# Score costs in the plan, fillers in score banks, 48-column chain matmuls, bf16 sums of heads and softmax steps on POOL in a two-layer decode kernel

## The chip, the cores and the metric

The kernel runs on one core of a Trainium2 chip. That core has five engines with a queue each: TensorE (PE, with its weight loads shown as PEld), VectorE (DVE), ScalarE (ACT), GpSimd (POOL) and SyncE (SP), which here only issues DMAs. Each queue is worked off in order; the engines wait for each other through semaphores. The metric is the device time of one execution in microseconds, lower is better.

## The reference

Eight sequences (rows) decode one token through four blocks: attention, MLP, the same attention, the same MLP. Attention has 16 query heads on 8 kv heads of size 256 over a cache of 4096 positions, and needs all of K and V (268 MB) in each of the two layers; the kernel keeps some units of K and V on the chip from a row's first layer to its second. Cut to what matters:

```python
def _A_ref(x, k_cache, v_cache, wq, wo):
    q = (x @ wq).reshape(B, Sq, 16, 256).transpose(0, 2, 1, 3)
    k = jnp.repeat(k_cache, 2, axis=1); v = jnp.repeat(v_cache, 2, axis=1)
    p = softmax(einsum("bhqd,bhkd->bhqk", q, k) * 256 ** -0.5)
    return einsum("bhqk,bhkd->bhqd", p, v).transpose(0, 2, 1, 3).reshape(B, Sq, 4096) @ wo
def _B_ref(x, w1, w2, w3, w4):        # x: (B, 1, 448)
    hs = (shifted gelu(layernorm(x) @ w1)) @ w2       # all shifted away: one position
    x1 = x + hs
    return x1 + gelu(layernorm(x1) @ w3) @ w4
x = x + _A_ref(layernorm(x), ...)
x = x + _B_ref(layernorm(x), ...)
x = x + _A_ref(layernorm(x), ...)
x = x + _B_ref(layernorm(x), ...)
```

With one position the shift by 1 or 2 places moves all of `h` out, so `hs` is zero and w1 and w2 are not read.

## The kernel before

**A plan makes the order.** The body first lists every operation with its engine, a duration, the keys it reads and writes, the PSUM banks it touches and a priority (`Plan.op`). `Plan.schedule` then goes through them by time and writes out one queue for each engine; `synchronise` puts in the semaphore waits. So a changed duration or a changed column count moves instructions in all queues. For PE an operation has two durations (clock warm and cold), the columns it streams and its number of matmuls. Where PE would be idle, the plan puts fillers in: matmuls of 512 columns on the identity, whose result nobody reads, as long as the columns of the last 3.413 us stay under `TARGET` (or `HOT`) and a bank of the four `psT` is free.

**The unit of work is a head**: one kv head with its two query heads, 8 heads x 8 rows x 2 layers = 128. `front(layer, b, h)` does:
- load K in four units of 512 KB, of which one DMA takes up to four; the buffer `kv` holds 30 units;
- transpose K on PE (L1185) into one of four `psT` banks, evicted by DVE (L1168) or ACT (L1169), whichever the plan finds free;
- scores (L999): matmuls of 512 columns into one of two score banks `psS`, four in the four row groups of the output at a time;
- the softmax: the maximum over the bank (L1020, DVE), `pw` (L1022, DVE) masks it by query head, an all-reduce over partitions on POOL gives `gm` (L1025), two small DVE steps make the bias `nb` (L1030, L1032), ACT takes exp with its row sum `lr` (L1035), PE turns `pr` into columns (`turn_p`, L1042), DVE copies them to `pT` (L1046), makes `rs` out of `lr` (L1050), POOL all-reduces it to `Db` (L1052), DVE takes the reciprocal `rc` (L1054).

`back(layer, b, h)` loads V, accumulates p times V in `psP` (L1078) in four row groups, copies the result to `oS` in f32 (L1089), sums the row groups with f32 matmuls (`sum_mm`, L1095) and scales by `rc` into `oA` (L1099). After the seventh head of a row `wo_rows` (L1119) applies wo to seven heads, after the eighth `wo_mm` to the last; then comes the MLP of the row (`mlp`, L825 to L941), whose result `x2c` gives the queries of the second layer (`second_queries`, L1246). Heads of the next rows are put around it.

**Queues.** POOL's queue has the two all-reduces of each head and the copies of layer 0's queries into `qz` (L966). The small matmuls of the chain (queries, MLP, wo) repeat their columns: `QW`, `HW` = 24 and `YW` = 12 columns are streamed where one is needed.

Of the kernel before, what the change touches and what calls it, by code (L numbers as in the profile page):

```python
# [6 lines left out]
P = 128  # L7
B = 8
D = 448
HKV = 8  # L10
DH = 256
F = 1792
NC5 = 5
# [22 lines left out]
BACKS = (0, 3, 6)  # L36
MIX = "KKKKKFFF"
QFIRST = 1
QW, HW, YW = 24, 24, 12
SC = 456  # L40
NQZ = 8
YC = 8
WO = 8
O2 = 0

# [29 lines left out]
class Plan:  # L75

    WIN, COLS, TARGET = 3.413, 3000, 3500

    HOT = 3500


    ISSUE, LEAD = 4.0, 5.0
# [375 lines left out]
def bass_interleave_layers__gqa_block_cached__mixer_s_mlp__decode_kernel(  # L460
# [410 lines left out]
    def mlp(src, skey, n, dst, dkeys):  # L871
# [48 lines left out]
        def y_mm(t):  # L920
            last = None
            for mt in range(NC5):
                for fc in range(14):
                    r = hT[:, fc * n:(fc + 1) * n]
                    r = r if yw == n else bcast(r, yw // n, 1)
                    last = dup(t, ch, yc + mt * yw, yw, w4_sb, fc * D, mt, r, fc == 0, fc == 13)
            return last
        pe(y_mm, 70, rd=["hT"] + W4, wr=[kb], banks=[bk], width=yw)
        ps4 = ch[:, yc:yc + NC5 * yw].rearrange("p (a n) -> p a n", n=yw)[:, :, 0:n]
        dv(lambda v: v.scalar_tensor_tensor(dst, ps4, 0.5, base[:, :, 0:n], ALU.mult, ALU.add),  # L930
           rd=[kb, "base"] + [("base", r) for r in range(1, n) if few], wr=dkeys, banks=[bk])

    def dup(t, dst, at, n, w, a, mt, rhs, start, stop):

# [20 lines left out]
    def front(layer, b, h, prio=None):  # L955
# [26 lines left out]
        for u in range(4):  # L982
            if u in fresh:
                for pc in range(2):
                    bank = transpose_piece(ks[u], pc, u in hold)
                    if u in hold:
                        held.setdefault(u, []).append(bank)

            if u % 2 == 0:
                continue  # L990

            def sc(t, u=u):
                last = None
                w = 2 - 2 * (u // 2)
                for c in range(2):
                    for g4 in range(4):
                        q = ks[u - 1 + g4 // 2]
                        r = 32 * g4
                        last = t.matmul(ps[r:r + 4, :], qz[zi][:, c, w:w + 4],  # L999
                                        slot_ap(q, g4 % 2 * 1024, 1024)[:, c:1024:2],  # L1000
                                        start=(u < 2 and c == 0), stop=(u >= 2 and c == 1),
                                        skip_group_check=True, tile_position=(0, r))
# [17 lines left out]
        plan.op("dve", lambda v: v.tensor_reduce(pm[nm][:, :], ps[:, :], axis=AX.X, op=ALU.max), 0.62,  # L1020
                "max", rd=scs, wr=[("pm", nm)], banks=[sk], prio=hi)
        plan.op("dve", lambda v: v.tensor_scalar(pw[nm][:, :], other[:, :], pm[nm][:, 0:1], 0.0, ALU.add,  # L1022
                                                 ALU.add), 0.1,
                "max", rd=[("pm", nm), "other"], wr=[("pw", nm)], prio=hi)
        plan.op("pool", lambda gp: gp.partition_all_reduce(gm[nm][:, :], pw[nm][:, :], P, RO.max),  # L1025
                0.46, "max", rd=[("pw", nm)], wr=[("gm", nm)], prio=hi)
# [3 lines left out]
        plan.op("dve", lambda v: v.tensor_tensor(nb[nm][:, 1:2], gm[nm][:, 1:2], eb[ei][:, 1:2], ALU.mult), 0.1,  # L1030
                "max", rd=[("gm", nm), ("eb", ei)], wr=[("nb1", nm)], prio=hi)
        plan.op("dve", lambda v: v.scalar_tensor_tensor(nb[nm][:, 0:1], gm[nm][:, 0:1], eb[ei][:, 0:1],  # L1032
                                                        nb[nm][:, 1:2], ALU.mult, ALU.add), 0.1,
                "max", rd=[("gm", nm), ("eb", ei), ("nb1", nm)], wr=[("nb", nm)], prio=hi)
        plan.op("act", lambda a: a.activation(pr[:, :], ps[:, :], ACT.Exp, bias=nb[nm][:, 0:1], scale=scale,  # L1035
                                              accum_out=lr[nm][:, 0:1]), 0.62, "exp",
                rd=[("nb", nm)] + scs + fk, wr=["pr", ("lr", nm)], banks=[sk], prio=hi)
# [7 lines left out]
        pe(turn_p, 4, rd=["pr", "selS"], wr=scs, banks=[sk], name="pturn", prio=hi)  # L1045
        plan.op("dve", lambda v: v.tensor_copy(  # L1046
            pT[nr][:, :, :].rearrange("p (x s) j -> p x s j", s=4),
            ps[:, 0:64].rearrange("p (s x j) -> p x s j", s=4, j=2)), 0.17, "exp", rd=scs,
            wr=[("pT", nr, 0), ("pT", nr, 1)], banks=[sk], prio=hi)
# [8 lines left out]
    def back(layer, b, h):  # L1058
# [12 lines left out]
        for u in range(4):  # L1071
# [26 lines left out]
        pe(sum_mm, 8, rd=["oS", "sel_f"], wr=["o2"], banks=[M], name="osum", prio=hi)  # L1098
# [14 lines left out]
        if k == HKV - 1:  # L1113
            def wo_rows(t):
                last = None
                for n, x in enumerate(heads[:HKV - 1]):
                    for i in range(4):
# [16 lines left out]
            def turn(t):  # L1134
                last = None
                for mt in range(NC5):
                    for w in range(2):
                        last = dup(t, psM, YC + mt * YW, YW, oW, w * D, mt,
                                   bcast(sel[:, 0:1], YW, 1), w == 0, w == 1)
                return last  # L1140
            pe(turn, 10, rd=["hb", "g1", "g2", "hT", "sel"], wr=["psM"], banks=[M], name="turn",
               prio=hi, width=YW)
            dv(lambda v: v.tensor_tensor(acc[layer][:, :], xin, psM[:, YC:YC + NC5 * YW:YW], ALU.add),
               rd=["psM", xk], wr=[ak], banks=[M], name="acc", prio=hi)
        if k == HKV:
            def wo_mm(t):
                last = None
                for mt in range(NC5):
                    for i in range(4):
                        last = dup(t, psM, YC + mt * YW, YW, wo_sb, (4 * h + i) * D, mt,  # L1150
                                   bcast(oT[:, i % 2, i // 2:i // 2 + 1], YW, 1), i == 0,
                                   i == 3)
# [64 lines left out]
    def mid(b, heads):  # L1217

        src = x2c[b % 2]
        mlp(x1c[b % 2], ("x1", b), 1, src[:, :, 0:1], [("x2", b)])  # L1220
        sums(src, ("x2", b), 1, SC + 53)
        second_queries(b, heads[0], None, lambda: dv(
            lambda v: v.tensor_single_scalar(mom2[b % 2][:, :], psM[:, SC + 53:SC + 56], 1.0 / D, ALU.mult),
            rd=["psM"], wr=[("mom2", b)], banks=[M]))
        for h in heads[1:]:
            second_queries(b, h, None)
# [224 lines left out]
```

## Time and profile before

| | |
|---|---|
| median of 3 runs | 1138.31 us (1125.2 to 1138.76) |
| profiled execution | 1128.62 us, span 1126.8 us |
| mean granted TensorE clock | 0.851 |
| bytes moved by DMA | 440.39 MB, mean 391 GB/s |
| POOL all-reduce gm (L1025) | 128 times, mean 354 ns |
| POOL all-reduce Db (L1052) | 128 times, mean 398 ns |
| POOL copy qz (L966) | 64 times, mean 189 ns |
| DVE pw, nb, nb, rs (L1022, L1030, L1032, L1050) | 128 times each, mean 222, 153, 218, 227 ns |
| PE filler (L1392) | 87 times, mean 488 ns |

The profile page lists busy time by engine, the span in 40 slices with a digit for the busy tenths, the chain of work that ended last (followed back from the end through whatever released each step), and groups of equal instructions by line, with the idle time of the engine ahead of them and what ended it. "issue" names idle time in which the engine waited for nothing that the profile shows. L numbers are lines of the kernel before.

### The profile page before, as it was taken

What the parts mean: (1) busy time and instruction counts of PE and PEld (TensorE: products, weight loads), DVE (VectorE), ACT (ScalarE), POOL (GpSimd) and SP (SyncE); (2) the same over time, 40 slices, a digit from 0 to 9 for tenths busy, and PEclk for the clock granted to TensorE, in tenths of its full rate; (3) what the DMA queues carried; (4) which work ended last, traced back from release to release, by engine and by line L of the source; (5) the groups of instructions that cost most, each with busy time, mean ns of one, the idle gap of its engine ahead of it and who ended that gap; (6) DMA issues with size and microseconds to landing.
All of it is one profiled execution on the core that took longest, in us unless ns stands there. A gap on an engine that the chain in (4) does not pass through costs nothing.

```text
span 1126.8 us, 30990 instructions
## 1 busy us (share of the span) xinstructions
PE 962.0 (85%) x13744; PEld 674.1 (60%) x13744; DVE 648.1 (58%) x2055; ACT 286.9 (25%) x578; POOL 109.3 (10%) x347
## 2 busy tenths in 40 slices
PE   5798888988888988888988888888898997898998
PEld 4466546665566755665556655656555774575664
DVE  4357445665556745576466655666555664466562
ACT  1133112231123402243022321233122340133230
POOL 0100011000101101001010101100011010101010
PEclk9789759888789968899599886999778996689698
DMA  9999999988999999999999989999999998999894
GB/s 352 409 425 405 390 393 427 426 344 316 400 427 424 417 342 426 425 425 398 347 425 425 425 355 363 426 425 421 372 400 426 424 379 316 424 421 383 318 406 178
DMA packets 47430, 440.39 MB, mean 391 GB/s; under 512 B 5040, under 2 KB 8256, under 8 KB 16960
## 3 DMA queue, kind: packets, MB, share of 16 engines
q1 hardware_dynamic: 47296, 438.41, 95.5%
q8 instruction: 108, 1.77, 0.6%
q14 instruction: 26, 0.21, 0.0%
HBM read 438.38 MB, written 0.01 MB: 389 GB/s over the span
## 4 chain that ended last, share of the span: by engine, by line
PE 69%; DVE 15%; DMA 7%; ACT 5%; issue 3%; POOL 1%; POOLq 0%; ACTq 0%
PE psT L1185 27%; PE psS L999 12%; PE psP L1078 11%; PE psM L1095 6%; DMA kv<-in_A_v_cache_dram 4%; ACT pr L1035 4%; DVE pm L1020 4%; DMA kv<-in_A_k_cache_dram 3%; PE psM L825 3%; PE psT L1392 2%; DVE oS L1089 2%; DVE kv L1168 2%; PE psM L938 2%; PE psM L1119 2%; PE psM L941 2%
## 5 line engine op out<-in xcount | busy, mean ns | idle before, releaser
L1185 PE MATMUL psT<-ident_f,kv 128*128 128x128 f32 x2816 | 384.2, 291 | 2.9 <-DMA kv<-in_A_k_cache_dram 2.8
L1185 PEld LDWEIGHTS psT<-ident_f,kv 128*128 128x128 f32 x2816 | 335.8, 150 | 64.8 <-issue 58.7
L1168 DVE COPY kv<-psT 128x512 f32<-128x512 f32 x425 | 289.0, 689 | 114.4 <-PE psT L1185 103.2
L1169 ACT COPY kv<-psT 128x512 f32<-128x512 f32 x311 | 181.2, 587 | 370.5 <-PE psT L1185 337.1
L1078 PE MATMUL psP<-kv,pT 128*2 128x256 bf16 x4096 | 186.6, 316 | 19.2 <-DVE pT L1046 11.6
L999 PE MATMUL psS<-kv,qz 128*4 128x512 bf16 x2048 | 173.9, 430 | 10.1 <-DVE kv L1168 7.9
L1095 PEld LDWEIGHTS psM<-self_f,oS 128*128 128x128 f32 x512 | 82.7, 227 | 89.2 <-DVE oS L1089 70.3
L1078 PEld LDWEIGHTS psP<-kv,pT 128*2 128x2 bf16 x4096 | 87.3, 89 | 66.6 <-DVE pT L1046 16.7
L1095 PE MATMUL psM<-self_f,oS 128*128 128x2 f32 x512 | 91.8, 284 | 41.0 <-DVE oS L1089 38.2
L1020 DVE TENSOR_REDUCE pm<-psS 128x1 f32<-128x512 f32 x128 | 88.2, 689 | 53.8 <-PE psS L999 53.2
L1035 ACT ACTIVATE pr<-psS,nb,fac 128x512 bf16<-128x512 f32 x64 | 49.8, 778 | 255.4 <-DVE nb L1032 252.9
L1025 POOL PARTITION_ALL_REDUCE gm<-pw x128 | 45.4, 354 | 443.1 <-DVE pw L1022 435.5
L1042 PE MATMUL psS<-selS,pr 128*128 128x16 bf16 x512 | 33.2, 173 | 59.4 <-ACT pr L1035 58.7
L1089 DVE COPY oS<-psP 128x256 f32<-128x256 f32 x128 | 53.9, 421 | 45.6 <-PE psP L1078 44.2
L1042 PEld LDWEIGHTS psS<-selS,pr 128*128 128x128 bf16 x512 | 23.3, 99 | 85.0 <-ACT pr L1035 73.6
L1052 POOL PARTITION_ALL_REDUCE Db<-rs x128 | 51.0, 398 | 227.3 <-DVE rs L1050 221.4
L999 PEld LDWEIGHTS psS<-kv,qz 128*4 128x4 bf16 x2048 | 36.3, 87 | 55.6 <-issue 33.2
L1035 ACT ACTIVATE pr<-psS,nb 128x512 bf16<-128x512 f32 x64 | 44.0, 688 | 90.3 <-DVE nb L1032 89.4
L1050 DVE TENSOR_SCALAR rs<-own,lr 128x2 f32<-128x2 f32 x128 | 29.1, 227 | 44.2 <-ACT pr L1035 43.2
L1099 DVE TENSOR_TENSOR oA<-psM,rc 128x4 bf16<-128x4 f32 x128 | 20.5, 160 | 51.4 <-PE psM L1095 50.7
L825 PEld LDWEIGHTS psM<-x2c,wq_sb 128*128 128x128 bf16 x768 | 30.6, 100 | 19.7 <-issue 9.1
L966 POOL COPY qz<-q1T 128x4 bf16<-128x4 bf16 x64 | 11.7, 189 | 306.2 <-PE psS L999 288.8
(158 smaller groups left out, 629.9 us busy)
## 6 DMA issues: line engine op xcount, KB each, us to landing
kv<-in_A_k_cache_dram SPq DMA_DIRECT2D x73, 2048.0 KB, 22.0
kv<-in_A_v_cache_dram SPq DMA_DIRECT2D x69, 2048.0 KB, 17.2
kv<-in_A_v_cache_dram SPq DMA_DIRECT2D x65, 1024.0 KB, 9.7
kv<-in_A_v_cache_dram SPq DMA_DIRECT2D x58, 512.0 KB, 5.9
kv<-in_A_k_cache_dram SPq DMA_DIRECT2D x27, 1024.0 KB, 11.6
wo_sb<-in_A_wo_dram SPq DMA_DIRECT2D x1, 3584.0 KB, 45.1
wq_sb<-in_A_wq_dram SPq DMA_DIRECT2D x3, 1024.0 KB, 16.4
kv<-in_A_k_cache_dram SPq DMA_DIRECT2D x6, 512.0 KB, 6.4
```

What stands on the lines that cost most here:

```text
L825: last = t.matmul(bank[:, at + i * step:at + i * step + copies], w, r, start=(kc == 0), stop=(kc == 3))
L999: last = t.matmul(ps[r:r + 4, :], qz[zi][:, c, w:w + 4], slot_ap(q, g4 % 2 * 1024, 1024)[:, c:1024:2], start=(u < 2 and c == 0), stop=(u > ...
L1020: plan.op("dve", lambda v: v.tensor_reduce(pm[nm][:, :], ps[:, :], axis=AX.X, op=ALU.max), 0.62, "max", rd=scs, wr=[("pm", nm)], banks=[sk ...
L1035: plan.op("act", lambda a: a.activation(pr[:, :], ps[:, :], ACT.Exp, bias=nb[nm][:, 0:1], scale=scale, accum_out=lr[nm][:, 0:1]), 0.62, "exp",
L1042: last = t.matmul(ps[:, 16 * i:16 * i + 16], pr[:, i * P:(i + 1) * P], selS[:, :], start=True, stop=True)
L1052: plan.op("pool", lambda gp: gp.partition_all_reduce(Db[nr][:, :], rs[nr][:, :], P, RO.add), 0.5, "sum", rd=[("rs", nr, 0), ("rs", nr, 1)] ...
L1078: last = t.matmul(ps[g4:g4 + 2, at:at + DH], pT[nr][:, i, :], slot_ap(q, s * 256, 256), start=(i < 4), stop=(i >= 28), skip_group_check=Tr ...
L1089: plan.op("dve", lambda v: v.tensor_copy(oS[:, :], ps[:, at:at + DH]), 0.36, "o", rd=[("pv", par, x) for x in range(4)], wr=["oS"], banks= ...
L1095: last = t.matmul(psM[:, O2 + 2 * c:O2 + 2 * c + 2], oS[:, c:DH:2], self_f[:, :], start=True, stop=True)
L1168: return e.tensor_copy(dst, psT[bank][:, :])
L1169: return e.copy(dst, psT[bank][:, :])
L1185: last = t.transpose(psT[bank][:, s * P:(s + 1) * P], src, ident_f[:, :])
```

## The change

Six edits, in the order of the title:
- The plan counts a group of eight score matmuls with 1024 columns and 0.36 us (warm) in place of 4096 and 0.5; `wo_rows` with 448 x 7 in place of 448 x 28. The plan's limits for columns go from 3000 and 3500 to 3200 and 3800.
- Fillers may also be written to a score bank, between the copy of pT and the bank's next scores.
- Chain matmuls stream 48 columns (`QW`, `HW`, `width_of` for the first two output tiles of `YW`) in place of 24 and 12; the columns in `psM` are laid out anew, and `psM` is cleared once more for each row and layer. `turn_p` streams 48 columns in place of 16.
- The sum of a head's row groups takes two bf16 words of `oS` (the value and what is left of it) with four bf16 matmuls of 24 columns, in place of two f32 matmuls of 2. The first word is copied by DVE or ACT, the second subtracted by DVE.
- `pw`, the two steps of `nb`, and `rs` go from DVE to POOL; the first step of `nb` now covers both columns.
- Some planned durations follow the measured ones.

```diff
-QW, HW, YW = 24, 24, 12
-SC = 456
+QW, HW, YW = 48, 48, 24
+SC = 192
-YC = 8
+YC = 32
...
-    WIN, COLS, TARGET = 3.413, 3000, 3500
-    HOT = 3500
+    WIN, COLS, TARGET = 3.413, 3200, 3800
+    HOT = 3800
...
-    oS = sb("oS", [P, DH], f32)
+    oS = sb("oS", [P, 2, DH], bf)
...
+    def width_of(mt):
+        return 2 * YW if mt < 2 else YW
...
-            o = plan.op("pe", sc, (0.5, 0.95, 4096, 8), "sc",
+            o = plan.op("pe", sc, (0.36, 0.72, 1024, 8), "sc",
...
+            if u == 1:
+                o.tbank = NT + par
...
-        plan.op("dve", lambda v: v.tensor_scalar(pw[nm][:, :], other[:, :], pm[nm][:, 0:1], 0.0, ALU.add,
-                                                 ALU.add), 0.1,
+        plan.op("pool", lambda v: v.tensor_scalar(pw[nm][:, :], other[:, :], pm[nm][:, 0:1], 0.0, ALU.add,
+                                                 ALU.add), 0.2,
...
-        plan.op("dve", lambda v: v.tensor_tensor(nb[nm][:, 1:2], gm[nm][:, 1:2], eb[ei][:, 1:2], ALU.mult), 0.1,
+        plan.op("pool", lambda v: v.tensor_tensor(nb[nm][:, :], gm[nm][:, :], eb[ei][:, :], ALU.mult), 0.19,
...
-        plan.op("dve", lambda v: v.scalar_tensor_tensor(nb[nm][:, 0:1], gm[nm][:, 0:1], eb[ei][:, 0:1],
-                                                        nb[nm][:, 1:2], ALU.mult, ALU.add), 0.1,
+        plan.op("pool", lambda v: v.tensor_tensor(nb[nm][:, 0:1], nb[nm][:, 0:1], nb[nm][:, 1:2], ALU.add), 0.19,
...
-                last = t.matmul(ps[:, 16 * i:16 * i + 16], pr[:, i * P:(i + 1) * P], selS[:, :], start=True,
-                                stop=True)
+                last = t.matmul(ps[:, 16 * i:16 * i + 48], pr[:, i * P:(i + 1) * P],
+                                bcast(selS[:, :], 3, 1), start=True, stop=True)
...
-        plan.op("dve", lambda v: v.tensor_scalar(rs[nr][:, :], own[:, :], lr[nm][:, 0:1], 0.0, ALU.mult, ALU.add),
-                0.1, "sum", rd=[("lr", nm), "own"], wr=[("rs", nr, 0), ("rs", nr, 1)], prio=hi)
+        plan.op("pool", lambda v: v.tensor_scalar(rs[nr][:, :], own[:, :], lr[nm][:, 0:1], 0.0, ALU.mult, ALU.add),
+                0.2, "sum", rd=[("lr", nm), "own"], wr=[("rs", nr, 0), ("rs", nr, 1)], prio=hi)
...
-        plan.op("dve", lambda v: v.tensor_copy(oS[:, :], ps[:, at:at + DH]), 0.36, "o",
-                rd=[("pv", par, x) for x in range(4)], wr=["oS"], banks=[bk], prio=hi)
+        plan.op("ev", hi_part, {"dve": 0.42, "act": 0.45}, "o", rd=pvs, wr=["oS0"], banks=[bk], prio=hi)
+        plan.op("dve", lambda v: v.tensor_tensor(oS[:, 1, :], po, oS[:, 0, :], ALU.subtract), 0.42, "o",
+                rd=["oS0"] + pvs, wr=["oS1"], banks=[bk], prio=hi)
...
-                last = t.matmul(psM[:, O2 + 2 * c:O2 + 2 * c + 2], oS[:, c:DH:2], self_f[:, :], start=True,
-                                stop=True)
+                for w in range(2):
+                    last = t.matmul(psM[:, O2 + 2 * c:O2 + 2 * c + 24], oS[:, w, c:DH:2],
+                                    bcast(sel[:, :], 12, 1), start=(w == 0), stop=(w == 1))
...
-            o = plan.op("pe", wo_rows, (1.4, 2.7, 448 * 28, 28), "wor",
+            o = plan.op("pe", wo_rows, (1.4, 2.7, 448 * 7, 28), "wor",
...
+            dv(lambda v: v.memset(psM[:, YC:YC + NC5 * YW], 0.0), 0.1, rd=["hb", "g1", "g2"], wr=["psM"], banks=[M],
+               name="acc", prio=hi)
...
-        dst, n = psT[bank][:, :], 512
+        dst, n = (psT[bank] if bank < NT else psS[bank - NT])[:, :], 512
```

In the built programs the queues change as follows: POOL from 347 counted instructions to four more for each head, with library loads (instructions without operands) ahead of those that need another library than the one before them; PE's fillers from 87 to 420; of the 128 first copies of `oS` 70 stay on DVE and 58 go to ACT.

More of the change, by code (lines that the diff above doesn't have):

```diff
@@ L924, in y_mm @@
                     r = hT[:, fc * n:(fc + 1) * n]
-                    r = r if yw == n else bcast(r, yw // n, 1)
-                    last = dup(t, ch, yc + mt * yw, yw, w4_sb, fc * D, mt, r, fc == 0, fc == 13)
+                    w = n if yw == n else width_of(mt)
+                    r = r if yw == n else bcast(r, w // n, 1)
+                    last = dup(t, ch, yc + mt * yw, w, w4_sb, fc * D, mt, r, fc == 0, fc == 13)
             return last
@@ L1018, in front @@
         scs = [("sc", par, x) for x in range(4)]
[L1020 removed]
+        plan.op("dve", lambda v: v.tensor_reduce(pm[nm][:, :], ps[:, :], axis=AX.X, op=ALU.max), 0.69,
                 "max", rd=scs, wr=[("pm", nm)], banks=[sk], prio=hi)
[L1022 to L1023 removed]
+        plan.op("pool", lambda v: v.tensor_scalar(pw[nm][:, :], other[:, :], pm[nm][:, 0:1], 0.0, ALU.add,
+                                                 ALU.add), 0.2,
                 "max", rd=[("pm", nm), "other"], wr=[("pw", nm)], prio=hi)
@@ L1029, in front @@
         ei = b % 2 if layer else 2
-        plan.op("dve", lambda v: v.tensor_tensor(nb[nm][:, 1:2], gm[nm][:, 1:2], eb[ei][:, 1:2], ALU.mult), 0.1,
+        plan.op("pool", lambda v: v.tensor_tensor(nb[nm][:, :], gm[nm][:, :], eb[ei][:, :], ALU.mult), 0.19,
                 "max", rd=[("gm", nm), ("eb", ei)], wr=[("nb1", nm)], prio=hi)
-        plan.op("dve", lambda v: v.scalar_tensor_tensor(nb[nm][:, 0:1], gm[nm][:, 0:1], eb[ei][:, 0:1],
-                                                        nb[nm][:, 1:2], ALU.mult, ALU.add), 0.1,
-                "max", rd=[("gm", nm), ("eb", ei), ("nb1", nm)], wr=[("nb", nm)], prio=hi)
+        plan.op("pool", lambda v: v.tensor_tensor(nb[nm][:, 0:1], nb[nm][:, 0:1], nb[nm][:, 1:2], ALU.add), 0.19,
+                "max", rd=[("nb1", nm)], wr=[("nb", nm)], prio=hi)
         plan.op("act", lambda a: a.activation(pr[:, :], ps[:, :], ACT.Exp, bias=nb[nm][:, 0:1], scale=scale,
-                                              accum_out=lr[nm][:, 0:1]), 0.62, "exp",
+                                              accum_out=lr[nm][:, 0:1]), 0.75, "exp",
                 rd=[("nb", nm)] + scs + fk, wr=["pr", ("lr", nm)], banks=[sk], prio=hi)
@@ L1041, in turn_p @@
             for i in range(4):
-                last = t.matmul(ps[:, 16 * i:16 * i + 16], pr[:, i * P:(i + 1) * P], selS[:, :], start=True,
-                                stop=True)
+                last = t.matmul(ps[:, 16 * i:16 * i + 48], pr[:, i * P:(i + 1) * P],
+                                bcast(selS[:, :], 3, 1), start=True, stop=True)
             return last
-        pe(turn_p, 4, rd=["pr", "selS"], wr=scs, banks=[sk], name="pturn", prio=hi)
+        pe(turn_p, 4, rd=["pr", "selS"], wr=scs, banks=[sk], name="pturn", prio=hi, width=48)
         plan.op("dve", lambda v: v.tensor_copy(
@@ L1048, in front @@
             ps[:, 0:64].rearrange("p (s x j) -> p x s j", s=4, j=2)), 0.17, "exp", rd=scs,
-            wr=[("pT", nr, 0), ("pT", nr, 1)], banks=[sk], prio=hi)
-        plan.op("dve", lambda v: v.tensor_scalar(rs[nr][:, :], own[:, :], lr[nm][:, 0:1], 0.0, ALU.mult, ALU.add),
-                0.1, "sum", rd=[("lr", nm), "own"], wr=[("rs", nr, 0), ("rs", nr, 1)], prio=hi)
+            wr=[("pT", nr, 0), ("pT", nr, 1)], banks=[sk], prio=hi).tbank = NT + par
+        plan.op("pool", lambda v: v.tensor_scalar(rs[nr][:, :], own[:, :], lr[nm][:, 0:1], 0.0, ALU.mult, ALU.add),
+                0.2, "sum", rd=[("lr", nm), "own"], wr=[("rs", nr, 0), ("rs", nr, 1)], prio=hi)
         plan.op("pool", lambda gp: gp.partition_all_reduce(Db[nr][:, :], rs[nr][:, :], P, RO.add),
@@ L1087, in back, with hi_part @@
                 o.frees = [vs[u]]
-        plan.op("dve", lambda v: v.tensor_copy(oS[:, :], ps[:, at:at + DH]), 0.36, "o",
-                rd=[("pv", par, x) for x in range(4)], wr=["oS"], banks=[bk], prio=hi)
+        po = ps[:, at:at + DH]
+        def hi_part(e):
+            return e.tensor_copy(oS[:, 0, :], po) if e is nc.vector else e.copy(oS[:, 0, :], po)
+        pvs = [("pv", par, x) for x in range(4)]
+        plan.op("ev", hi_part, {"dve": 0.42, "act": 0.45}, "o", rd=pvs, wr=["oS0"], banks=[bk], prio=hi)
+        plan.op("dve", lambda v: v.tensor_tensor(oS[:, 1, :], po, oS[:, 0, :], ALU.subtract), 0.42, "o",
+                rd=["oS0"] + pvs, wr=["oS1"], banks=[bk], prio=hi)
         def sum_mm(t):
@@ L1094, in sum_mm @@
             for c in range(2):
-                last = t.matmul(psM[:, O2 + 2 * c:O2 + 2 * c + 2], oS[:, c:DH:2], self_f[:, :], start=True,
-                                stop=True)
+                for w in range(2):
+                    last = t.matmul(psM[:, O2 + 2 * c:O2 + 2 * c + 24], oS[:, w, c:DH:2],
+                                    bcast(sel[:, :], 12, 1), start=(w == 0), stop=(w == 1))
             return last
-        pe(sum_mm, 8, rd=["oS", "sel_f"], wr=["o2"], banks=[M], name="osum", prio=hi)
+        pe(sum_mm, 4, rd=["oS0", "oS1", "sel"], wr=["o2"], banks=[M], name="osum", prio=hi, width=24)
         plan.op("dve", lambda v: v.tensor_tensor(
@@ L1137, in turn @@
                     for w in range(2):
-                        last = dup(t, psM, YC + mt * YW, YW, oW, w * D, mt,
-                                   bcast(sel[:, 0:1], YW, 1), w == 0, w == 1)
-                return last
+                        last = dup(t, psM, YC + mt * YW, width_of(mt), oW, w * D, mt,
+                                   bcast(sel[:, 0:1], width_of(mt), 1), w == 0, w == 1)
+                return last
+            dv(lambda v: v.memset(psM[:, YC:YC + NC5 * YW], 0.0), 0.1, rd=["hb", "g1", "g2"], wr=["psM"], banks=[M],
+               name="acc", prio=hi)
             pe(turn, 10, rd=["hb", "g1", "g2", "hT", "sel"], wr=["psM"], banks=[M], name="turn",
@@ L1149, in wo_mm @@
                     for i in range(4):
-                        last = dup(t, psM, YC + mt * YW, YW, wo_sb, (4 * h + i) * D, mt,
-                                   bcast(oT[:, i % 2, i // 2:i // 2 + 1], YW, 1), i == 0,
+                        last = dup(t, psM, YC + mt * YW, width_of(mt), wo_sb, (4 * h + i) * D, mt,
+                                   bcast(oT[:, i % 2, i // 2:i // 2 + 1], width_of(mt), 1), i == 0,
                                    i == 3)
@@ L1220, in mid @@
         mlp(x1c[b % 2], ("x1", b), 1, src[:, :, 0:1], [("x2", b)])
-        sums(src, ("x2", b), 1, SC + 53)
+        sums(src, ("x2", b), 1, SC + 64)
         second_queries(b, heads[0], None, lambda: dv(
-            lambda v: v.tensor_single_scalar(mom2[b % 2][:, :], psM[:, SC + 53:SC + 56], 1.0 / D, ALU.mult),
+            lambda v: v.tensor_single_scalar(mom2[b % 2][:, :], psM[:, SC + 64:SC + 67], 1.0 / D, ALU.mult),
             rd=["psM"], wr=[("mom2", b)], banks=[M]))
```

## The prediction

> **What bounds the kernel now.** I read the page first (totals, slices, chain), then the POOL engine's timeline, because the change moves work there, then the groups of instructions for durations.
>
> ```profile
> PE 962.0 (85%) x13744; PEld 674.1 (60%) x13744; DVE 648.1 (58%) x2055; ACT 286.9 (25%) x578; POOL 109.3 (10%) x347
> ...
> DMA  9999999988999999999999989999999998999894
> ```
>
> From the page's totals and slices. The 16 DMA engines are nearly full from start to end and PE works 85% of the span; POOL does almost nothing, and its 347 instructions are the smallest number.
>
> ```profile
> PE 69%; DVE 15%; DMA 7%; ACT 5%; issue 3%; POOL 1%; POOLq 0%; ACTq 0%
> ```
>
> From the chain that ended last: PE's work, handed on by DVE, sets the end close to what DMA can deliver. POOL is 1% of it, about 11 us. So POOL has slack, if what is moved there costs what POOL's instructions cost now. What they can cost stands in its timeline (start, duration, engine, line; in brackets the idle time before and what ended it):
>
> ```profile
> 1.69 0.10 POOL L652 MEMSET xf<- 128x5 bf16 x1
> 12.65 0.28 POOL L657 TENSOR_SCALAR_AFFINE_SELECT ident_f<-ident_f 128x128 f32<-128x128 f32 x1 [10.85 <-issue]
> ...
> 32.91 0.19 POOL L966 COPY qz<-q1T 128x4 bf16<-128x4 bf16 x1 [1.55 <-PE psS L999]
> ...
> 39.41 0.37 POOL L1025 PARTITION_ALL_REDUCE gm<-pw  x1 [6.31 <-issue]
> ...
> 40.22 0.35 POOL L1025 PARTITION_ALL_REDUCE gm<-pw  x1 [0.30 <-DVE pw L1022]
> ```
>
> Twice POOL stands still with nothing to wait for: 10.85 us ahead of its first affine select, 6.31 us ahead of its first all-reduce. The input of that all-reduce, pw, was ready at 33.84:
>
> ```profile
> 33.61 0.23 DVE L1022 TENSOR_SCALAR pw<-other,pm 128x2 f32<-128x2 f32 x1
> ...
> 39.81 0.16 DVE L1030 TENSOR_TENSOR nb<-gm,eb 128x1 f32<-128x1 f32 x1 [5.24 <-POOL gm L1025]
> ```
>
> The second all-reduce, at 40.22, starts without a pause. In the built program of before, POOL's queue has a library load (an instruction with no operands) at exactly these two places and nowhere else: library 0 ahead of the affine select, library 1 ahead of the first all-reduce. The later 255 all-reduces and all the copies between them need none. So the two pauses are the price of a library load.
>
> **The change: library loads.** The change puts tensor_scalar (pw, rs) and tensor_tensor (nb, twice) on POOL, between the two all-reduces of each head. In the built program of after, these four carry a load of library 0 ahead of them wherever an all-reduce came before, and each all-reduce a load of library 1. POOL's order for one head is: load 0, pw, load 1, all-reduce gm, load 0, nb, nb, rs, load 1, all-reduce Db. That is 4 loads for each of the 128 heads (8 kv heads, 8 rows, 2 layers); counted over the queue, 512 in place of 2. One (library 0 ahead of the affine select) lies in the start as before; 511 are counted below. They are in POOL's queue in order, so nothing behind them can pass.
>
> One load is taken at 6.31 us, the all-reduce row. Lower end 5.57 us: if the load had not counted until pw was there (39.41 - 33.84). Upper end 10.85 us for a load of library 0, whose only row holds the program's start as well. I take 6.31 for both libraries, since the later row is free of the start. It was measured while the DMA engines were full (share 1.01 from 33.1 to 39.4); with POOL slow they will be mostly idle, and if the load competes for them it could fall, at most to half (3.2 us) if it took turns with one busy queue. Sum: 511 x 6.31 = 3224 us.
>
> [...]
>
> **POOL's own work for one head.** Two all-reduces 0.354 + 0.398 us (their groups). The four small steps were never on POOL; nearest row the POOL copy of 128x4, 189 ns, bounds 98 ns (a POOL memset) and 282 ns (the affine select): 4 x 0.19 = 0.76. Between nb and rs POOL must wait for exp on ACT: in before nb ended at 40.23, rs began at 41.08, 0.85 us. This is a wait put into POOL's queue: the load and the Db all-reduce of the same head, and everything of the next head, stand behind it. Together 2.36 us; x128 = 302 us. The 64 qz copies of layer 0, which stand in the same queue, add 64 x 0.19 = 12 us.
>
> So one head takes POOL 4 x 6.31 + 2.36 = 27.6 us, where the whole kernel now takes 1126.8 / 128 = 8.8 us for one. POOL becomes the bound by a factor of three. Two things are not covered by it:
>
> *Start and end.* Up to the first pw, 33.6 us; after the last Db, which ended at 1097.3, the last rows' work to the span's end, 29.5 us. Both stay.
>
> *Where POOL waits for the others.* Scores of the next head need a score bank (two), free once pT of two heads ago is copied; that is half a head's POOL time (13 us) ahead of need, and all of PE's work comes to 962 / 128 = 7.5 us a head. DVE now stands behind rc, which waits for Db: at most six evictions (6 x 0.689 = 4.1 us) and the maximum (0.69 us) follow before the next pw, and a load of library 0 (6.31 us) covers them. What stays is the change of layer in each of 8 rows, where the MLP needs the last Db and the next scores need the MLP: before, POOL idled 18.09 to 23.45 us there, 157.7 us over 8; one load in each hides 6.31, so 157.7 - 50.5 = 107 us are added. With PE's clock lower it could be twice that.
>
> **Everything else in the change** shortens or lengthens engines that now have three times the time they need, and is counted at zero under POOL. What it would cost uncovered:
> - Fillers 87 to 420: 333 x 488 ns = 162 us of PE, in its idle time.
> - Chain matmuls with 48 columns: 8 columns take 166 ns, 24 take 184; so about 27 ns more at 48, and up to 30 us over some 2,000 matmuls.
> - The sums of heads in bf16: four matmuls took 0.63 to 1.01 us in f32, the four bf16 ones of pturn 0.27, so some 50 us less PE; 128 subtractions of 0.42 us more, and 58 of the 128 copies go from DVE to ACT.
> - DVE loses 222 + 153 + 218 + 227 = 820 ns a head, 105 us in all; with the sums about 75 us net.
> - Score matmuls at 1024 columns in place of 4096, the new limits 3200 and 3800, and fillers in free score banks only change which fillers are put where.
> - The clearing of psM, 16 x about 0.11 us.
>
> PE's 962 us at a granted clock of 0.851 would be 1640 at 0.5: still under half of POOL's time.
>
> **Sum**, against the profiled execution (1128.62 us, span 1126.8, so 1.8 around it; 0.9% under the median 1138.31, which is nothing here): 33.6 + 3224 + 302 + 12 + 107 + 29.5 + 1.8 = 3710 us, of which 486 are not loads. Forecast 3710.
>
> **Rivals.**
> 1. *Library 0 is dearer.* For: 10.85 us in its only row. Against: that row includes the start of the program. 256 x 10.85 + 255 x 6.31 + 486 = 4873 us; halfway, 4290.
> 2. *Loads are cheaper on an idle memory.* For: the measured one ran with DMA full. Against: nothing shows that it shares its path. At 3.2 us: 511 x 3.2 + 486 = 2121; at 5 us: 3041.
> 3. *A load is paid only once (the other side: faster).* If both libraries stayed in place after their first use, the 511 loads cost next to nothing. For: no row shows the same library loaded twice. Against: each load asks for the library that the one before it replaced, so there is nothing in place to find. It decides once a load costs less than (1126.8 - 33.6 - 29.5 - 302 - 12 - 107) / 511 = 1.26 us, when POOL falls below the others. Then DVE's part of the chain (15%, 169 us) shrinks by 75 / 648, 20 us, PE runs warmer, and DMA sets the floor: 438 MB at the 425 GB/s of the full slices is 1032 us, with the tail of 29.5 about 1062. Between 1062 and 1107 and some relief on PE: 1090 us, 4% less.
> 4. *The small steps cost more on POOL than a copy does*, at 1 us each: 128 x 4 x 0.81 = 415 more, 4125 us.
>
> **How the numbers follow.** Chances: forecast (a load of 5.6 to 7 us) 0.56; rival 1 0.19; rival 2 0.17; rival 3 0.05; rival 4 0.03. A difference of 2% is what can be told here. Slower needs any of the first four: 0.95. Rival 3 divides into 0.035 faster and 0.015 the same. Range 3000 to 4650: from loads of 5 us up to most of rival 1; left out are rival 3, the lower half of rival 2 and the top of rival 1, together under 0.2.
>
> **What would show it.** POOL idle with "issue" as its reason some 500 times at about 6 us, that wait at the head of the list; the chain on POOL and its queue; 27 to 28 us from one gm to the next; DMA slices at 2 to 4 tenths, some 120 GB/s (438 MB / 3.7 ms); PE busy under 40%, with a granted clock nearer the 0.50 of the thin matmuls from 145 to 165 us than the mean 0.85. Wrong would be: idle times under 1.26 us ahead of these steps (rival 3); pauses of 10 us ahead of pw and nb but 6 ahead of the all-reduces (rival 1); both near 3 to 5 (rival 2); POOL durations near 1 us (rival 4).

## The result and the profile after

| | before | after |
|---|---|---|
| median | 1138.53 us (4 runs) | 4378.81 us (4362.98 to 4380.22, 4 runs) |
| ratio | | 3.853, 95% interval 3.822 to 3.883 |
| span of the profiled execution | 1126.8 us | 4361.2 us |
| mean granted TensorE clock | 0.851 | 0.608 |

The kernel became 3.85 times slower. The same three lines of the page as before, now of the changed kernel (busy time of each engine; DMA's busy tenths over 40 slices; the chain that ended last by engine):

```profile
PE 1288.0 (30%) x14077; PEld 811.0 (19%) x14077; DVE 595.2 (14%) x1631; ACT 306.7 (7%) x634; POOL 231.4 (5%) x859
...
DMA  7123321232212232122221222222232212312230
...
issue 73%; PE 13%; DVE 6%; POOL 5%; ACT 2%; DMA 0%; POOLq 0%; SPq 0%
```

No engine is busy for even a third of the span. That is the first thing to see: a kernel bound by something that no busy time shows. 73% of the chain is "issue", time in which an engine stood still and waited for nothing on record. The list of waits says which engine (who waited for whom: us in total, times, longest):

```profile
POOL pw L1029 <- issue: 847.7, 91, 12.3
POOL gm L1032 <- issue: 807.6, 128, 10.8
POOL nb L1037 <- issue: 791.1, 112, 8.7
POOL Db L1058 <- issue: 761.7, 128, 7.7
POOL pw L1029 <- DVE pm L1027: 276.9, 28, 19.2
POOL qz L971 <- PE psS L1004: 256.0, 35, 18.2
...
POOL rs L1056 <- issue: 109.3, 11, 11.8
POOL rs L1056 <- ACT pr L1041: 107.2, 115, 1.0
...
POOL nb L1039 <- issue: 57.4, 8, 7.8
```

The six rows with "issue" add up to 3374.8 us, 77% of the span, all on POOL, and always ahead of a step that needs another library than the one before it. One head in POOL's timeline:

```profile
639.41 0.41 POOL L1058 PARTITION_ALL_REDUCE Db<-rs  x1 [5.99 <-issue]
646.98 0.19 POOL L971 COPY qz<-q1T 128x4 bf16<-128x4 bf16 x1 [7.16 <-PE psS L1004]
657.81 0.30 POOL L1029 TENSOR_SCALAR pw<-other,pm 128x2 f32<-128x2 f32 x1 [10.65 <-issue]
663.88 0.37 POOL L1032 PARTITION_ALL_REDUCE gm<-pw  x1 [5.76 <-issue]
671.27 0.18 POOL L1037 TENSOR_TENSOR nb<-gm,eb 128x2 f32<-128x2 f32 x1 [7.01 <-issue]
671.53 0.19 POOL L1039 TENSOR_TENSOR nb<-nb 128x1 f32<-128x1 f32 x1
672.73 0.26 POOL L1056 TENSOR_SCALAR rs<-own,lr 128x2 f32<-128x2 f32 x1 [1.01 <-ACT pr L1041]
678.76 0.41 POOL L1058 PARTITION_ALL_REDUCE Db<-rs  x1 [5.77 <-issue]
```

Four pauses in 39 us, each ahead of 0.2 to 0.4 us of work. Between them the second nb and rs, ahead of which the built program has no load, start without one. The copy ahead of pw has no load either, but waits 7.16 us for the other engines, and the 10.65 us of the load behind it begin only then: that turns out to matter.

### The profile page after: what moved, and what is told of

Its sections match the earlier page's. It is cut to its first block, busy times and chain, and to the rows that moved or that the text cites. A ratio compares the mean times of both kernels' runs of the same rounds, so it can differ in the third digit from the quotient of the medians.

```text
span 4361.2 us, 32831 instructions
## 1 busy us (share of the span) xinstructions
PE 1288.0 (30%) x14077; PEld 811.0 (19%) x14077; DVE 595.2 (14%) x1631; ACT 306.7 (7%) x634; POOL 231.4 (5%) x859
## 4 chain that ended last, share of the span: by engine, by line
issue 73%; PE 13%; DVE 6%; POOL 5%; ACT 2%; DMA 0%; POOLq 0%; SPq 0%
PE psT L1200 5%; PE psS L1004 3%; ACT pr L1041 2%; PE psP L1084 2%; DVE kv L1183 2%; DVE pm L1027 1%; POOL Db L1058 1%; POOL gm L1032 1%; PE psM L825 1%; POOL pw L1029 1%; DVE oS L1101 1%; POOL rs L1056 1%; PE psS L1407 1%; PE psM L943 1%; POOL nb L1039 1%
## 5 line engine op out<-in xcount | busy, mean ns | idle before, releaser
L1048 PE MATMUL psS<-selS,pr 128*128 128x48 bf16 x512 | 43.7, 216 | 2395.7 <-ACT pr L1041 2395.7
L1200 PE MATMUL psT<-ident_f,kv 128*128 128x128 f32 x2816 | 524.6, 356 | 98.2 <-DVE kv L1183 97.7
L1200 PEld LDWEIGHTS psT<-ident_f,kv 128*128 128x128 f32 x2816 | 448.9, 187 | 196.3 <-DVE kv L1183 108.3
L1052 DVE CAST pT<-psS 128x64 bf16<-128x64 f32 x128 | 28.5, 223 | 2254.7 <-PE psS L1048 2254.7
L1084 PE MATMUL psP<-kv,pT 128*2 128x256 bf16 x4096 | 225.2, 363 | 54.6 <-DVE pT L1052 47.1
L1004 PE MATMUL psS<-kv,qz 128*4 128x512 bf16 x2048 | 210.7, 511 | 79.0 <-DVE kv L1183 49.2
L1108 PE MATMUL psM<-sel,oS 128*128 128x24 bf16 x512 | 35.4, 183 | 351.2 <-DVE oS L1101 345.2
L1029 POOL TENSOR_SCALAR pw<-other,pm 128x2 f32<-128x2 f32 x128 | 39.0, 304 | 1172.5 <-issue 847.7
L1407 PE MATMUL psS<-ident_f 128*128 128x512 bf16 x249 | 100.8, 498 | 0.0
L1032 POOL PARTITION_ALL_REDUCE gm<-pw x128 | 47.5, 371 | 807.6 <-issue 807.6
L1407 PE MATMUL psT<-ident_f 128*128 128x512 bf16 x171 | 72.4, 544 | 0.0
```

Source lines behind the costliest of these rows:

```text
L1004: last = t.matmul(ps[r:r + 4, :], qz[zi][:, c, w:w + 4], slot_ap(q, g4 % 2 * 1024, 1024)[:, c:1024:2], start=(u < 2 and c == 0), stop=(u > ...
L1029: plan.op("pool", lambda v: v.tensor_scalar(pw[nm][:, :], other[:, :], pm[nm][:, 0:1], 0.0, ALU.add, ALU.add), 0.2, "max", rd=[("pm", nm), ...
L1048: last = t.matmul(ps[:, 16 * i:16 * i + 48], pr[:, i * P:(i + 1) * P], bcast(selS[:, :], 3, 1), start=True, stop=True)
L1084: last = t.matmul(ps[g4:g4 + 2, at:at + DH], pT[nr][:, i, :], slot_ap(q, s * 256, 256), start=(i < 4), stop=(i >= 28), skip_group_check=Tr ...
L1200: last = t.transpose(psT[bank][:, s * P:(s + 1) * P], src, ident_f[:, :])
```

## The experiments

Two theories at first: the library loads are the whole loss; or small steps are slow to hand to POOL, whatever they load. A third question was what the rest of the change does without them. In what follows "a load" is a library load, counted in the built program.

**Steps back on DVE, all else of the change kept (2 loads).**

```diff
-        plan.op("pool", lambda v: v.tensor_scalar(pw[nm][:, :], other[:, :], pm[nm][:, 0:1], ...), 0.2,
+        plan.op("dve", lambda v: v.tensor_scalar(pw[nm][:, :], other[:, :], pm[nm][:, 0:1], ...), 0.1,
...
```
(and the same for both steps of nb and for rs)

> The changed kernel with pw, both steps of nb and rs back on DVE; all else of the change kept, so POOL's queue holds two library loads again. If the loads are the whole loss: 1062 to 1130 us, about 1090, with POOL idle under issue only twice. If the longer PE queue (fillers 87 to 420, 48 columns, bf16 sums) also costs: over 1160 us.

1105.44 us, ratio to before 0.971 (0.968 to 0.974). Taking the four steps back removes the whole loss, and the rest of the change is a gain of 2.9%. From its page:

```profile
PEclk9899999999999999999999999999999999999898
DMA  9999999998999999999999999999999999999893
...
PE 46%; DMA 39%; DVE 8%; ACT 3%; issue 3%; POOL 1%; SPq 0%; POOLq 0%; DVEq 0%
```

PE's clock is now nearly always full (mean 0.976), and DMA's share of the chain went from 7% to 39%: the kernel has become more of a DMA kernel. Whether still more clock would bring more, no run shows.

**The four steps alone on the kernel before (512 loads).**

```diff
-        plan.op("dve", lambda v: v.tensor_scalar(pw[nm][:, :], ...), 0.1,
+        plan.op("pool", lambda v: v.tensor_scalar(pw[nm][:, :], ...), 0.2,
...
```
(and nb, nb, rs as in the change)

> The kernel before with nothing but the four steps on POOL, 512 loads. If the loads are the whole loss: within 3% of the changed kernel's 4379 us, and some 3375 us of POOL idle under issue. If the other edits share in it: under 4100 us.

4375.97 us (one execution), the changed kernel's time within 0.1%; its rows under "issue" add up to 3431 us. So the four steps are sufficient as well as necessary, and what the other edits gain is lost under POOL.

**The steps as copies on POOL (2 loads).** Same engine, shapes, waits and place in the queue, but an operation that needs no library; the maximum's mask, the bias and the sum of the softmax are left out.

```diff
-        plan.op("pool", lambda v: v.tensor_scalar(pw[nm][:, :], other[:, :], pm[nm][:, 0:1], ...), 0.2,
+        plan.op("pool", lambda v: v.tensor_copy(pw[nm][:, :], own[:, :]), 0.2,
-        plan.op("pool", lambda v: v.tensor_tensor(nb[nm][:, :], gm[nm][:, :], eb[ei][:, :], ALU.mult), 0.19,
+        plan.op("pool", lambda v: v.tensor_copy(nb[nm][:, :], eb[ei][:, :]), 0.19,
...
```

> The changed kernel with each of the four steps on POOL replaced by a copy of the same shape with the same waits: the copies need no library. The arithmetic of the softmax's maximum and sum is left out. If the loads are the whole loss: like the run with the steps back on DVE within 3%, 1060 to 1150 us. If it is the hand-over of small steps to POOL, its launch or its order in the queue: over 1500 us.

1106.74 us, ratio 0.971 (0.967 to 0.974), no different from the steps on DVE. The groups of its POOL (count, busy us, mean ns, idle before and its cause):

```profile
L1057 POOL PARTITION_ALL_REDUCE Db<-rs x128 | 50.9, 398 | 11.2
L1031 POOL PARTITION_ALL_REDUCE gm<-pw x128 | 45.4, 354 | 16.8 <-issue 6.3
L1038 POOL COPY nb<-nb 128x1 f32<-128x1 f32 x128 | 24.5, 192 | 7.2
L1029 POOL COPY pw<-own 128x2 f32<-128x2 f32 x128 | 23.7, 185 | 384.0 <-DVE pm L1027 348.7 <-DVE rsi L717 20.1 <-DVE oA L1111 5.7
```

"issue" is back to the two loads of the kernel before (6.3 us ahead of the first gm, 11.8 ahead of the affine select), and otherwise only real waits are left. This separates the two theories: the loads are the cause, not the hand-over. It also says what the moved steps could have been worth. DVE's busy time is 603.4 us in place of the 659.1 with the steps on DVE; that is less than the 105 us of the four steps, in part because DVE has 44 copies out of PSUM here that ACT does there. The kernel is not faster for it (1106.74 against 1105.44).

**One step alone, in two places (256 or so loads).**

```diff
 rs alone: pw and both nb back on DVE
 pw alone: both nb and rs back on DVE
```

> The changed kernel with only rs on POOL: two loads a head, 257 or so, both inside the softmax of the head (ahead of rs and of Db). Loads as the bound: 128 x (7.0 + 5.9) = 1651 us under issue, plus the head's other work and POOL's wait for the next scores, 2200 to 2800 us, about 2600. If the time came from handing small steps to POOL and not from the loads: one step of four moved, so about 1090 + 3290 / 4 = 1910 us.

> The changed kernel with only pw on POOL: 256 loads, as many as with rs alone (2880 us), but the load of library 0 now stands where POOL waits for the next scores anyway. If a load costs nothing while POOL waits: 128 x (9.5 + 0.3 + 6.0 + 0.4 + 2.6) = 2400, so 2000 to 2600 us. If the number of loads alone decides: 2880 us within 3%.

2879.74 and 2829.71 us. The first is above its range, the second well above; the count of loads predicted the second one (within 3% of the first). The first missed by the price: its loads took 8.75 us ahead of rs and 7.12 ahead of Db on average (988.5 and 912.0 us under "issue" in 113 and 128 pauses), where 7.0 and 5.9 were put in. That a load costs nothing where POOL waits anyway did not hold. The groups of pw alone show why:

```profile
L1029 POOL TENSOR_SCALAR pw<-other,pm 128x2 f32<-128x2 f32 x128 | 39.0, 304 | 1206.5 <-issue 858.2 <-DVE pm L1027 321.9 <-DVE rsy L719 19.6
L971 POOL COPY qz<-q1T 128x4 bf16<-128x4 bf16 x64 | 11.5, 187 | 345.2 <-PE psS L1004 327.6 <-DVE q1T L1307 17.5
```

POOL spends its wait for the scores in the copy qz (327.6 us), and only then does the load behind it begin. By the timeline, 45 of the 94 open pauses ahead of pw (480 of the 858.2 us) stand directly behind such a copy, and no load that stands there is hidden. The other 49 have no copy ahead of them: there the maximum was ready before the load was through, so there was no wait to hide in. So in POOL's order the loads hid only behind waits that stand after them (31 pauses ahead of pw, put down to pm, 321.9 us).

**Loads that belong to nothing (257 loads).** Steps on DVE; after each Db a step on a scratch tile that nobody reads.

```diff
+        plan.op("pool", lambda v: v.tensor_scalar(junk[:, :], own[:, :], 2.0, 0.0, ALU.mult, ALU.add), 0.2,
+                "junk", rd=["own", ("Db", nr), "junk"], wr=["junk"], prio=hi)
```

> The kernel with the steps back on DVE, plus one step on a scratch tile on POOL after each Db, which nothing reads: 257 loads, none of them inside a softmax, no step of the computation moved. If POOL's occupation by loads is the cause: 2200 to 2900 us, near the 2830 and 2880 us of the runs with one moved step and as many loads. If what counts is that loads stand inside the softmax's chain: under 1500 us.

2508.82 us: more than twice the time, although no step of the computation moved. Not quite as the expectation has it, 23 of the 128 heads do have a pair of loads between their gm and their Db, because the queue puts the step of another head there (169.3 us under "issue" ahead of Db); the other 105 heads have none. Most of the loads thus lie outside the softmax, and the time more than doubles even so: it is POOL's time that runs out (1947.6 of the 2507.0 us of the span under "issue"). With the step inside the softmax of every head (the two runs above) as many loads cost 321 to 371 us more.

**The copies of qz on DVE (512 loads).**

```diff
-            plan.op("pool", lambda gp: gp.tensor_copy(
+            plan.op("dve", lambda gp: gp.tensor_copy(
                 qz[zi][:, :, 2:4], ...
```

> The changed kernel with the 64 qz copies on DVE in place of POOL; 512 loads as before. If the copies, waiting for scores in POOL's queue, held back the load behind them (256 us of such waits): 4130 to 4250 us. If that wait only changes its name: 4379 us within 1%.

4209.69 us, 169 us less, within the first range. The wait in the copy did hold the load behind it back; where the copy is gone, the load runs during the same wait:

```profile
L1029 POOL TENSOR_SCALAR pw<-other,pm 128x2 f32<-128x2 f32 x128 | 39.2, 306 | 1092.4 <-issue 477.8 <-DVE pm L1027 425.3 <-DVE rsy L719 74.6
```

In the changed kernel this group had 847.7 under issue and 276.9 under pm. Not all of the 256 us came back: the load ahead of gm now took 7.38 us on average (945.2 / 128) where it had taken 6.31 (807.6 / 128).

**The plan told what a load costs (420 loads).**

```diff
 planned us: pw 0.2 -> 7.3, both all-reduces 0.46 and 0.5 -> 6.3, first nb 0.19 -> 7.2
```

> The changed kernel with the planned durations of the POOL steps raised to what they take with a load (pw 7.3, all-reduces 6.3, nb 7.2 us); the plan then puts steps of two heads under one load (420 loads) and orders the other queues around it. If only the number of loads counts: 1105 + 418 x 6.42 = 3790 us. If the queues' order also held POOL up (its 550 us of waiting for scores and maxima): 3100 to 3600 us.

3482.26 us, in the second range. Its "issue" rows add up to 2929 us in 408 pauses, 7.2 each, and 3480.5 - 2929 = 552 us of the span lie outside them, against 4361.2 - 3374.8 = 986 in the changed kernel. Both remainders still hold the loads under pauses that the profile puts down to other engines, 11 here and 33 there: at 7.2 and 7.0 us, an estimate, 79 and 231 us. So what is no load fell from some 755 to 473 us. Much of what went is waiting for PE: the copies of qz wait for PE 77 us in all instead of 256,

```profile
L971 POOL COPY qz<-q1T 128x4 bf16<-128x4 bf16 x64 | 11.1, 181 | 94.7 <-PE psS L1004 77.1 <-DVE q1T L1306 17.5
```

and the wait of pw for pm, 276.9 us in the changed kernel, is no longer among the larger causes of its idle time. So the plan's order, made with a POOL step of 0.2 us, was itself worth some 280 us of loss, by this estimate; the other 600 us are the 92 loads that the new order saves.

**The price of a load by itself.** Steps on DVE, six pairs of loads at the start, while DMA fills the buffers, and six after the last result.

```diff
+    for i in range(6):
+        plan.op("pool", lambda v: v.tensor_scalar(junk[:, :], own[:, :], 2.0, 0.0, ALU.mult, ALU.add), 0.2, ...
+        plan.op("pool", lambda gp: gp.partition_all_reduce(self_f[:, :], junk[:, :], P, RO.max), 0.4, ...
```

> The kernel with the steps back on DVE, plus six pairs of a library-0 step and an all-reduce on a scratch tile at the start, while DMA fills the buffers, and six pairs after the last result, when DMA has nothing left. If the price of a load depends on DMA: 10 to 11 us (library 0) and 8 to 10 us (library 1) in the first 60 us, 7.0 and 5.7 us at the end. If it depends only on the library: 7.0 and 5.7 us at both places, within 0.5 us.

POOL's timeline, two pairs with DMA full (share 0.99 from 14 to 60 us), the next one, by when the transfers were done, and two at the end (share 0.00 from 1160 us):

```profile
33.29 0.18 POOL L684 TENSOR_SCALAR junk<-own 128x2 f32<-128x2 f32 x1 [8.62 <-issue]
40.85 0.37 POOL L686 PARTITION_ALL_REDUCE self_f<-junk  x1 [7.37 <-issue]
50.96 0.18 POOL L684 TENSOR_SCALAR junk<-own 128x2 f32<-128x2 f32 x1 [9.74 <-issue]
58.45 0.37 POOL L686 PARTITION_ALL_REDUCE self_f<-junk  x1 [7.31 <-issue]
65.64 0.18 POOL L684 TENSOR_SCALAR junk<-own 128x2 f32<-128x2 f32 x1 [6.82 <-issue]
71.77 0.37 POOL L686 PARTITION_ALL_REDUCE self_f<-junk  x1 [5.95 <-issue]
...
1188.66 0.18 POOL L1412 TENSOR_SCALAR junk<-own 128x2 f32<-128x2 f32 x1 [6.87 <-issue]
1194.81 0.37 POOL L1414 PARTITION_ALL_REDUCE self_f<-junk  x1 [5.96 <-issue]
1202.83 0.18 POOL L1412 TENSOR_SCALAR junk<-own 128x2 f32<-128x2 f32 x1 [7.65 <-issue]
1209.07 0.37 POOL L1414 PARTITION_ALL_REDUCE self_f<-junk  x1 [6.05 <-issue]
```

Only the first three pairs met a full DMA; the other three at the start ran with a share of 0.01 or less and cost what those at the end do. That makes a comparison inside one run, with nothing else at work (stretch, length, busy us of PE, PEld, DVE, ACT and POOL, granted clock, DMA share, GB/s):

```profile
33.50:40.80 7.30, 0.00 (x0) 0.00 (x0) 0.00 (x0) 0.00 (x0) 0.00 (x0) 0.50 1.01 426
66.00:71.70 5.70, 0.00 (x0) 0.00 (x0) 0.00 (x0) 0.00 (x0) 0.00 (x0) 0.50 0.00 0
```

Both theories of it are half right. The library counts (7.2 against 6.0 us on average over the quiet loads), and so does DMA: in the pairs shown 1.3 to 2.6 us more, less than the 3 to 4 expected for library 0. The very first load of library 1, ahead of the step at 24.29, took 10.60. The whole execution took 1238.22 us.

**Where the 2.9% come from.**

```diff
 plan's edits alone, on the kernel before: score columns 4096 -> 1024, wo_rows 28 -> 7 x 448, limits 3200 / 3800, fillers in psS
 the rest alone: the kernel with the steps back on DVE, less those edits (48 columns and bf16 sums stay)
```

> The kernel before with the plan's edits alone: score matmuls counted as 1024 columns, wo_rows as 7 x 448, limits 3200 and 3800, fillers in score banks (398 fillers in place of 87). If the 2.9% that the change gives without the moved steps comes from these: 1100 to 1115 us, with a granted clock over 0.95. If it comes from the 48 columns and the bf16 sums: 1130 to 1145 us.

> The kernel with the steps back on DVE, less the plan's edits: 48 columns and bf16 sums stay, 99 fillers. If the plan's edits carry the 2.9%: 1125 to 1145 us, granted clock near 0.85. If columns and sums carry it: 1100 to 1115 us.

1123.75 us (ratio 0.990, 0.986 to 0.995) and 1118.44 us (0.988, 0.984 to 0.992): neither is where either theory put it. Each half gives about 1%. The product, 0.990 x 0.988 = 0.978, does not reach 0.971, but the two intervals together reach from 0.970 to 0.987, so it is not shown that the halves help each other. The mean granted clock rose with both, 0.94 and 0.91 against 0.851 before and 0.976 together. That they act through it is argued, not shown: with the columns and sums PE also has less to do (910.5 us busy in place of 962.0). The granted clock in tenths, the plan's edits alone first, then the rest alone:

```profile
PEclk9899899998899988999799999999799998999698
```

```profile
PEclk9799778998999988998799998999889998899899
```

The kernel with the steps on DVE has 9 nearly everywhere; each half alone leaves dips. The version that beats both kernels is that one, 1105.44 us. The columns and the bf16 sums were not taken apart.

## Why the prediction was right, and where it was off

It said 3710 us, 3000 to 4650, slower with 0.95; the median is 4378.81, 18% above the forecast. The mechanism, the queue and the place are as forecast; the size was held by the range, not by the sum. Term by term, against the profiled execution (4362.98 us, 653 above the sum):

| term | predicted us | measured us |
|---|---|---|
| 511 loads | 3224 | 3375 under issue, some 231 more under waits (estimate) |
| POOL's steps and the wait for exp | 302 + 12 | 220 busy + 107 for exp + 12 |
| POOL waits for scores and maxima | 107 | 256 for scores, some 94 for maxima (estimate) |
| up to the first pw | 33.6 | 35.8 |
| after the last Db | 29.5 | 27.4 |

*How the loads are counted.* The 3375 us lie in 478 open pauses of 7.06 us each, where 6.31 was predicted. The other 33 of the 511 loads, ahead of pw, lie in pauses that the profile puts down to DVE (28 of them to pm), 325 us in all and none under 6.78. Each is long enough to hold a whole load. At 7.0 us, what a load of library 0 took here with DMA quiet, that is 231 us of loads and 94 of true waiting; this is the estimate in the table. The prediction counted hidden loads in the same way.

*The term that was mis-sized most*, and so the first step that failed, is "I take 6.31 for both libraries": some 3606 us of loads are 382 more than the sum had, over half of the miss. The 256 loads of library 1 took 6.13 us on average (gm 6.31, Db 5.95), close to it. The 222 open loads of library 0 took 8.13 (pw 9.31, rs 9.94, nb 7.07). Two things make the difference, each read in the open pauses by the DMA share of the pause. Library 0 is dearer in quiet, by 1.1 us: at a share under 0.05 it took 7.03 us on average (132 pauses) and library 1 5.91 (163). And both took longer where DMA was busy: at a share of 0.6 and more, 10.7 (56 pauses) and 7.8 us (24). In the windows of the changed kernel's timeline above (the columns as in the run on the price):

```profile
647.20:657.80 10.60, 2.67 (x50) 0.91 (x38) 1.41 (x4) 0.00 (x0) 0.00 (x0) 0.91 0.95 373
658.10:663.90 5.80, 0.00 (x0) 0.00 (x0) 0.00 (x0) 0.00 (x0) 0.04 (x2) 0.50 0.05 23
664.20:671.30 7.10, 0.00 (x0) 0.00 (x0) 0.00 (x0) 0.00 (x0) 0.09 (x2) 0.50 0.00 0
```

the load of library 0 ahead of pw took 10.65 us while DMA was 95% busy, that ahead of nb 7.01 with no DMA at all, and library 1 between them 5.76. The open loads ahead of pw met a DMA share of 0.57 on average, those ahead of nb 0.03; that the next K is set free by the same scores would explain it, but no run tests that. Nor does a run show why library 1 under a full DMA took 6.31 in one place and 10.60 in another.

*Rival 1* (library 0 is dearer) was therefore nearer than the forecast: its halfway value, 4290 us, is 2% under the measured time, in part by luck: it has library 0 at 8.6 us and the waits still at 107. I had discounted its only row, 10.85 us, because it "holds the program's start as well". The run with the loads that belong to nothing speaks against that:

```profile
2.29 0.29 POOL L658 TENSOR_SCALAR_AFFINE_SELECT ident_f<-ident_f 128x128 f32<-128x128 f32 x1 [0.50 <-POOL xf L653]
```

It has the same start and the same load of library 0 there, and paused for 0.50 us, where all the other kernels paused for 10.49 to 11.79. It is also the only one whose last load is of library 0; whether that is the reason, no run tests. But the start alone does not take 10.85 us, and with a DMA share of 0.95 in that pause the row was within what loads of library 0 took later. *Rival 2* (cheaper on an idle memory) has the direction right, but the 6.31 row lay at the low end for a full DMA, and an idle one gave 5.9.

*The second step that failed* is "a load of library 0 (6.31 us) covers them", in the part on POOL waiting for the others: 107 us predicted, some 350 measured. I had counted the evictions that stand on DVE behind rc, but not what stands ahead of the load in POOL's own queue: the copy qz of layer 0, which I priced at 0.19 us and not at its wait for scores (256 us). The run with the copies on DVE gives 169 us back. The remaining 25 us or so of the miss are POOL's steps, pw and rs above all. So the two large errors had the same sign, and the time came inside the range because the range reached up to most of rival 1; the scenario that I gave 0.56, loads of 5.6 to 7 us, was just missed.

*Rival 3* (a load is paid once) is refuted: 128 loads ahead of gm and 128 ahead of Db, each with its pause. *Rival 4* (steps dearer on POOL, at 1 us): 185 to 304 ns, near the copy's 189; wrong.

*The edits counted at zero* were worth 0 under POOL (4375.97 without them, 4378.81 with them), as said, and 2.9% in the open; my estimate for the change with free loads, 1090 us, compares with 1106.74 for the copies on POOL. It took 20 us off for DVE, and the runs show nothing for it. Two slips in the working changed nothing: of the 511 loads 255 are of library 0 and 256 of library 1, not the other way round, and 27 ns more for 2,000 matmuls are 54 us, not 30.

*The signs.* As forecast: "issue" heads POOL's waits, with 478 such pauses in the six rows, the longest 12.3 us; PE busy 30% (under 40) at a clock of 0.608. A little lower than forecast: DMA at 1 to 3 tenths and 101 GB/s (2 to 4 and 120 expected). Not as forecast: one gm to the next 4361.2 / 128 = 34 us on average, not 27 to 28. The sign for rival 1 (10 us ahead of pw and nb, 6 ahead of the all-reduces) showed in part: 9.31 ahead of pw, but 7.07 ahead of nb.

## What to carry to other kernels

POOL's 10% busy time left room for 512 copies more (1106.74 us, ratio 0.971), but not for the 510 loads more that came with the same steps as arithmetic (4378.81 us, ratio 3.853). So before moving an operation, look in the built program for what comes with it (here a library load at each change between an all-reduce and arithmetic), and price the pair, not the operation. Here the price stood in the profile before, as a pause without a reason ahead of the first all-reduce (6.31 us; the 478 open pauses after took 7.06 each); multiply such a pause by how often it would recur. And list what stands ahead of a cost in its queue, with its waits: the copies ahead of the loads waited 256 us for scores, and with the copies on DVE the kernel was 169 us faster.

## What the runs showed of the hardware

With DMA quiet a load of library 0 took 7.03 us on average (changed kernel, share under 0.05, 132 pauses) and 7.2 (run on the price, 6.82 to 7.78), one of library 1 5.91 (163 pauses) and 6.0 (5.85 to 6.13). With a DMA share of 0.9 and more library 0 took 7.4 to 12.3 us (changed kernel, 27 pauses, 10.6 on average); for library 1 the row of the kernel before gave 6.31 and the first one of the run on the price 10.60. POOL's copies came with no load (steps as copies, 2 loads, each of the four groups at 184 to 192 ns). With the four steps alone on the kernel before, PE's matmuls are nearly the same as before (13762 against 13744), yet its busy time was 1278.4 us against 962.0, at a mean granted clock of 0.575 against 0.851; the same transposes took 366 ns in place of 291. So PE's busy times in these two runs can't be compared as work.
